# Chunked attention feeding an ELU network: the later tiles' attention as 64x64x64 products in four quarters of the array

## The chip, the cores and the metric

The kernel runs on one core of one Trainium2 chip. What is compared is the device time of one execution in microseconds (us), as the median of several. Beside it stands one execution that the hardware profiler took: when each engine worked, and what released it when it waited. TensorE (PE in the profile) multiplies matrices out of SBUF into the banks of PSUM; PEld is its weight load. VectorE (DVE), ScalarE (ACT) and GpSimd (POOL) do the elementwise work, and SyncE (SP) issues the DMAs.

## The reference

Attention runs inside chunks of 64 tokens: eight batches, eight heads, 576 tokens, head size 64. Its result, 4608 tokens by 512, goes through a two-layer network with an ELU between.

```python
q_c, k_c, v_c = [t.reshape(B, H, 9, 64, 64) for t in (q, k, v)]
scores = (1 / 8) * q_c @ k_c.transpose(0, 1, 2, 4, 3)
scores = scores - max(scores, axis=-1)
attn = exp(scores)
attn = attn / (sum(attn, axis=-1) + 1e-9)
x = (attn @ v_c) laid out as 4608 tokens x 512
h = x @ w_in                                   # 512 x 2048
g = where(h > 0, h, exp(min(h, 0)) - 1)
out = g @ w_out                                # 2048 x 512
```

## The kernel before

**Tiles and blocks.** A tile is 128 tokens, two chunks of 64. There are 36 tiles in nine blocks of four. The attention of the first four tiles runs at the start, that of the next four during block 0 (`early_tile`); both turn q, k and the attention weights with TensorE. The 28 others are the *later tiles* (`later_tile`): their q and k arrive by DMA in an order in which VectorE's 32x32 transposes turn them, and no TensorE transpose is needed. The attention of a tile is prepared one to two tiles ahead of the block that uses it.

**The network.** In blocks 0 to 2 (`hidden`, `elu`, `project`) each product is three products of float32r parts (high by high, high by low, low by high), all recorded at the helper's line L406. From block 3 on (`Pair`) two columns of `w_in` tiles are done at once by seven products instead of eight (`p1` to `p7`), whose operands were written to `a_dram` and are loaded again for every pair. Its parts are written as `o<-wo_hi,wi_hi` (second layer) and `h<-...` (first layer) in the profile.

**A later tile, step by step.** `attention_tile` is a generator; each `yield` ends a step, and the strings `LATER` and `PAIRS` say where a step stands (`n` a step of the following tile, `a` a step of the present one). The steps are these.

- VectorE turns q into `qT` (L283) and k into `k_apart` (L286), the latter in two instructions of 64 partitions each: head 2h in the upper half of the rows, head 2h+1 in the lower half, in separate columns, and zeros elsewhere.
- *Scores* (L357): for each pair of heads and each chunk one product with 128 rows, 64 output partitions and 128 columns. The zeros of `k_apart` keep the two heads apart. Eight products for a tile.
- The maximum `mx` (L363) and the subtraction (L377) on VectorE, the exponential (L381) on ScalarE, the sum, its inverse and the scaling (L383 to L316) on VectorE.
- Eight DMAs (L328) within SBUF bring `ah` into `aq`, and two VectorE transposes of 64 partitions (L333) put it into `a_apart`, which is zero where the chunks would mix.
- *Products by v* (L341): for each head one product with 128 rows, 64 output partitions and 128 columns. Eight for a tile.
- ScalarE copies the result out of PSUM into `xf` (`keep_x`, L392).

Scores and products by v each take a bank of their own from the pool `ps_a` of two. In nearly every tile the scores of the next tile and the products by v of the present one follow each other on TensorE.

**What sets the order.** All four engines run in the order in which the program is written (`manual_schedule`); waits are semaphores that the framework adds.

Of the kernel before, what the change touches and what calls it, by code (L numbers as in the profile page):

```python
# [10 lines left out]
F32 = mybir.dt.float32  # L11
# [9 lines left out]
def kernel(  # L21
# [59 lines left out]
    a_apart = const.tile([P, H, P], F32, name="a_apart")  # L81
# [178 lines left out]

    def front_tensor(q_sb, k_sb, kbd, at, psum):
# [16 lines left out]
        yield qT  # L278

    def front_vector(qk, kbd, at):  # L280
        yield
        qT = at.tile([P, NK, P], F32, name="qT")
        nc.vector.transpose(out=qT.rearrange("p h (t u) -> p h u t", u=4), in_=qk[:, 0])  # L283
        for j in range(2):
            js = slice(j * D, (j + 1) * D)
            nc.vector.transpose(  # L286
                out=kbd[js, :, j, :].rearrange("p h (t u) -> p h u t", u=4), in_=qk[js, 1]
            )
        yield qT
# [23 lines left out]
    def back_vector(a, z, v_sb, at, psum):  # L313

        ah = wst.tile([P, 2, H, Q], F32, name="y")
        nc.vector.tensor_tensor(  # L316
            out=ah.rearrange("p e h k -> p h e k"),
            in0=a.rearrange("p h (e k) -> p h e k", e=2),
            in1=z.rearrange("p h (e k) -> p h e k", e=1).broadcast_to([P, H, 2, Q]),
            op=ALU.mult,  # L320
        )
        yield
        aq = wst.tile([P, 2, H, Q], F32, name="y")
        for c in range(2):
            for e in range(2):
                for u in range(2):
                    p0, n0 = c * C + e * Q, c * C + u * Q
                    nc.sync.dma_start(out=aq[p0:p0 + Q, u], in_=ah[n0:n0 + Q, e])  # L328
        yield

        for c in range(2):
            cs = slice(c * C, (c + 1) * C)
            nc.vector.transpose(  # L333
                out=a_apart[cs, :, cs].rearrange("p h (u t) -> p h u t", u=2),
                in_=aq[cs].rearrange("p u h k -> p h u k"),
            )
        yield
        x_ps = psum([P, NK, P])
        for h in range(H):
            hp, j = divmod(h, 2)  # L340
            nc.tensor.matmul(  # L341
                x_ps[j * D:(j + 1) * D, hp, :], lhsT=v_sb[:, h, :], rhs=a_apart[:, h, :],
                start=True, stop=True,
            )
        return x_ps

    def attention_tile(tt: int, front, back, v_sb, kbd, at, psum, put, by_head: bool = False):
# [38 lines left out]
        x_ps = yield from back(a, z, v_sb, at, psum)  # L386
        yield
        put((slice(None), slice(None), slice(tt * P, (tt + 1) * P)), x_ps)
        yield
# [338 lines left out]
    with (  # L728
# [17 lines left out]
        for tt in range(NTT):  # L746
            psum = psum_of(ps_start)
            front = front_tensor(loaded[f"q{tt}"], loaded[f"k{tt}"], kbds[tt], start, psum)
            tiles.append(attention_tile(
                tt, front, back_tensor, loaded[f"v{tt}"], kbds[tt], start, psum, split_x  # L750
            ))
# [9 lines left out]
    ps_a = ctx.enter_context(tc.tile_pool(name="ps_a", bufs=2, space=bass.MemoryType.PSUM))  # L761
# [3 lines left out]
    psum = psum_of(ps_a)  # L765
# [19 lines left out]
    upcoming, second_products = None, []  # L785
# [6 lines left out]
    def early_tile(n: int):  # L792
# [4 lines left out]
        return attention_tile(  # L797
            n % NTT, front, back_tensor, load_v(n0, io), k_apart, at, psum, keep_x, by_head=True
# [11 lines left out]
    def later_tile(n: int, qk, v_sb):  # L810
        front = front_vector(qk, k_apart, at)
        return attention_tile(n % NTT, front, back_vector, v_sb, k_apart, at, psum, keep_x)
# [162 lines left out]
```

## Time and profile before

| | us |
|---|---|
| median of 3 runs | 890.68 (890.2 to 891.88) |
| the profiled execution | 890.75 |
| its span, first to last instruction | 889.0 |
| mean granted TensorE clock | 0.998 |
| VectorE busy | 554.5 |
| ScalarE busy | 486.2 |
| 28 transposes of q (L283) | 30.9 |
| 56 half transposes of k (L286) | 61.3 |
| 56 half transposes of the weights (L333) | 39.3 |

The first three rows differ by what lies around the span: 890.75 less 889.0 is 1.75 us before the first and behind the last instruction. A row of the profile gives an instruction's engine, its line, what it writes and reads, its shape, how often, and how long. A TensorE shape such as `128*64 128x128` means 128 rows of the array, 64 output columns of it, and a result of 128 columns. One product of float32 operands is issued as two matmul instructions (and two weight loads): 28 later tiles with eight products by v are 448 instructions at L341. The recorded length of a matmul is longer than its share of the array, since matmuls overlap; what counts is the distance between starts.

### The profile page before, as it was taken

The page shows a single profiled execution, that of the slowest core. Times are in us where ns is not written, and L with a number is a line of the kernel's source. Part 1 is how long each engine was busy: PE and PEld are TensorE (multiplying, and loading weights), DVE is VectorE, ACT ScalarE, POOL GpSimd, SP SyncE. Part 2 cuts the span into 40 slices and gives each one's busy share as a digit, 9 for nine tenths or more (in the row PEclk, how much of TensorE's full clock was granted, in tenths as well). Part 3 has the DMA queues.
Part 4 walks back from the last instruction along what each step waited for, and adds up shares of the span by engine and source line. Part 5 has one row for each costly group of instructions (what it writes and reads, how often), then busy time and mean ns, then how long its engine had stood idle before and what let it go on. Part 6 is the DMA issues. An engine that isn't in the chain of part 4 may idle for free.

```text
span 889.0 us, 15432 instructions
## 1 busy us (share of the span) xinstructions
PE 869.5 (98%) x5726; PEld 750.1 (84%) x5726; DVE 554.5 (62%) x859; ACT 486.2 (55%) x931; POOL 232.1 (26%) x196
## 2 busy tenths in 40 slices
PE   7899999999999999999999999999999999999997
PEld 6678887888888878888888888888888888888996
DVE  5899878567756586557655675567556755543222
ACT  5899984444544346455644564456444654465443
POOL 2000005114223023223422351226222622253221
PEclk9999999999999999999999999999999999999999
DMA  8775552545466758777689769876868688467521
GB/s 203 203 259 178 183 133 92 169 140 177 129 201 218 216 169 263 238 236 228 203 259 295 238 190 270 255 212 196 282 204 258 198 272 254 153 209 234 166 83 49
DMA packets 156700, 180.35 MB, mean 203 GB/s; under 512 B 67024, under 2 KB 123344, under 8 KB 156624
## 3 DMA queue, kind: packets, MB, share of 16 engines
q1 hardware_dynamic: 156624, 179.36, 65.9%
q8 instruction: 45, 0.74, 0.3%
q14 instruction: 31, 0.25, 0.1%
HBM read 147.85 MB, written 24.12 MB: 193 GB/s over the span
## 4 chain that ended last, share of the span: by engine, by line
PE 84%; DVE 5%; DMA 3%; SPq 2%; issue 2%; ACT 2%; POOL 1%; DVEq 0%; POOLq 0%; ACTq 0%
PE o L406 39%; PE h L406 37%; PE ps_a L357 3%; PE ps_a L341 3%; DMA st<-in_moe_w_out_dram 2%; DVE t L577 2%; SPq L230 1%; SPq L219 1%; POOL wi_lo L628 1%; POOL wi_lo L572 1%; DVE k_apart L286 1%; DVE e L620 0%; SPq L119 0%; DVE a L377 0%; DVE e L426 0%
## 5 line engine op out<-in xcount | busy, mean ns | idle before, releaser
L628 POOL TENSOR_TENSOR wi_lo<-e,wi_hi 128x512 fp32r<-128x512 f32 x94 | 123.2, 1311 | 336.8 <-ACT wi_hi L625 336.8
L406 PE MATMUL h<-xhi,wi_hi 128*128 128x256 f32 (+1 forms) x704 | 189.4, 315 | 1.4 <-DVE e L426 0.8
L613 DVE TENSOR_TENSOR kept<-h,kept 128x256 f32<-128x256 f32 x144 | 60.9, 423 | 169.5 <-PE h L406 122.1
L608 ACT COPY kept<-h 128x256 f32<-128x256 f32 x192 | 70.2, 366 | 168.1 <-PE h L406 167.9
L406 PE MATMUL o<-wo_lo,wi_hi 128*128 128x512 f32 x384 | 152.4, 397 | 0.0
L406 PE MATMUL o<-wo_hi,wi_hi 128*128 128x512 f32 x384 | 152.2, 396 | 0.0
L406 PE MATMUL o<-wo_hi,wi_lo 128*128 128x512 f32 x384 | 150.0, 390 | 1.0 <-POOL wi_lo L628 1.0
L406 PE MATMUL h<-xlo,wi_hi 128*128 128x256 f32 (+1 forms) x448 | 147.1, 328 | 0.0
L406 PEld LDWEIGHTS h<-xhi,wi_hi 128*128 128x128 f32 x704 | 123.6, 188 | 18.4 <-issue 4.3
L406 PE MATMUL h<-xhi,wi_lo 128*128 128x256 f32 (+1 forms) x448 | 131.4, 330 | 0.2 <-DVE wi_lo L160 0.2
L620 DVE SCALAR_TENSOR_TENSOR e<-e,kept 128x512 f32<-128x512 f32 x96 | 70.7, 736 | 38.7 <-ACT e L618 36.4
L406 PEld LDWEIGHTS h<-xlo,wi_hi 128*128 128x128 f32 x448 | 84.3, 188 | 12.0 <-DVE xlo L399 0.2
L406 PEld LDWEIGHTS h<-xhi,wi_lo 128*128 128x128 f32 x448 | 79.8, 188 | 11.9 <-issue 1.0
L406 PEld LDWEIGHTS h<-wi_lo,wi_hi 128*128 128x128 f32 x576 | 81.5, 189 | 9.5 <-ACT kept L608 1.0
L406 PEld LDWEIGHTS o<-wo_hi,wi_lo 128*128 128x128 f32 x384 | 72.3, 188 | 18.7 <-POOL wi_lo L628 2.7
L617 ACT ACTIVATE e<-kept 128x512 f32<-128x512 f32 x96 | 60.6, 632 | 48.7 <-DVE kept L613 41.8
L406 PE MATMUL h<-wi_lo,wi_hi 128*128 128x256 f32 x576 | 84.6, 282 | 0.3 <-ACT kept L608 0.3
L481 POOL TENSOR_TENSOR kept<-wi_hi,wi_lo 128x512 f32<-128x512 f32 x16 | 20.3, 1293 | 221.7 <-DVE qT L283 136.7
L406 PE MATMUL o<-wo_hi,ghi 128*128 128x512 f32 x192 | 76.4, 398 | 0.0
L406 PEld LDWEIGHTS o<-wo_lo,wi_hi 128*128 128x128 f32 x384 | 73.5, 191 | 2.3
L406 PE MATMUL o<-wo_hi,glo 128*128 128x512 f32 x192 | 75.0, 391 | 0.0
L406 PE MATMUL o<-wo_lo,ghi 128*128 128x512 f32 x192 | 74.9, 390 | 0.0
(90 smaller groups left out, 1444.8 us busy)
## 6 DMA issues: line engine op xcount, KB each, us to landing
wi_hi<-a_dram SPq DMA_DIRECT2D x128, 448.0 KB, 5.5
wi_lo<-a_dram SPq DMA_DIRECT2D x64, 448.0 KB, 5.7
kept<-in_q_dram SPq DMA_DIRECT2D x100, 128.0 KB, 7.0
kept<-in_k_dram SPq DMA_DIRECT2D x100, 128.0 KB, 5.2
st<-in_moe_w_in_dram SPq DMA_DIRECT2D x16, 512.0 KB, 4.2
st<-in_moe_w_out_dram SPq DMA_DIRECT2D x16, 512.0 KB, 4.9
a_dram<-kept SPq DMA_DIRECT2D x16, 512.0 KB, 4.1
y<-y SPq DMA_DIRECT2D x224, 32.0 KB, 1.9
```

The source lines that it names most:

```text
L219: nc.sync.dma_start(out=dst[p0:p0 + n], in_=src[b, :, s0:s0 + n, :].rearrange("h s d -> s h d"))
L230: nc.sync.dma_start(out=v_sb[j * C:(j + 1) * C, :, c, :], in_=v[b, j::2, ss, :].rearrange("h s d -> s h d"),)
L341: nc.tensor.matmul(x_ps[j * D:(j + 1) * D, hp, :], lhsT=v_sb[:, h, :], rhs=a_apart[:, h, :], start=True, stop=True,)
L357: nc.tensor.matmul(s_ps[cs, 2 * hp:2 * hp + 2, :], lhsT=qT[:, hp, cs], rhs=kbd[:, hp, :, cs], start=True, stop=True,)
L406: nc.tensor.matmul(ps, lhsT=a, rhs=b, start=start, stop=stop, skip_group_check=onto)
L481: nc.gpsimd.tensor_tensor(out=out, in0=a, in1=b, op=op)
L577: nc.vector.tensor_tensor(out=to, in0=a, in1=b, op=ALU.subtract)
L608: nc.scalar.copy(out=out, in_=self.x)
L613: nc.vector.tensor_tensor(out=out, in0=self.y, in1=self.kept[kept], op=ALU.add)
L617: nc.scalar.activation(out=e, in_=c, func=AF.Relu, scale=-1.0)
L620: nc.vector.scalar_tensor_tensor(out=e, in0=e, scalar=-1.0, in1=c, op0=ALU.add, op1=ALU.max)
L628: engine.tensor_tensor(out=glo, in0=e, in1=ghi.bitcast(F32), op=ALU.subtract)
```

## The change

The later tiles get a generator of their own, `later_attention`; the early ones keep theirs under the name `early_attention`, with the same instructions.

- k is turned by one transpose of 128 partitions into a dense `kT` (in the memory of `k_apart`), without zeros.
- The scores are sixteen products of 64 rows, 64 output partitions and 64 columns. They go round the four quarters of the array: (row half, output half) = (0,0), (1,1), (0,1), (1,0).
- The attention weights are turned by one transpose of 128 partitions into `turned`. `a_apart` and its memset go.
- The products by v are sixteen products of the same size over the same quarters.
- `ps_a` is one tile of two banks. A product whose rows are the upper half of the array writes the first bank, the others the second. The scores take columns 0 to 255 of both banks, the products by v columns 256 to 511. `banks[0]` is the tile last taken, so a tile's products by v stand in the banks that the next tile's scores took just ahead of them.
- Heads are kept in the order even, odd within `a` and `turned`, and the copy to `xf` reads from the two banks (128x2x4x64 in place of 128x4x128).

```diff
-    a_apart = const.tile([P, H, P], F32, name="a_apart")
+    turned = const.tile([P, H, C], F32, name="turned")
...
-    def front_vector(qk, kbd, at):
...
-    def back_vector(a, z, v_sb, at, psum):
...
+    def later_attention(tt: int, qk, v_sb):
+        halves = [slice(i * C, (i + 1) * C) for i in range(2)]
+        quarters = [(0, 0), (1, 1), (0, 1), (1, 0)]
+        yield
+        qT = at.tile([P, NK, P], F32, name="qT")
+        kT = k_apart.rearrange("p h j t -> p (h j) t")[:, :NK, :]
+        for i, to in enumerate((qT, kT)):
+            nc.vector.transpose(out=to.rearrange("p h (t u) -> p h u t", u=4), in_=qk[:, i])
+        yield
+        banks[:] = [ps_a.tile([P, 2, DM], F32, name="ps_a")]
+        scores = banks[0][:, :, :NK * C].rearrange("p j (h t) -> p j h t", h=NK)
+        for hp in range(NK):
+            for j, c in quarters:
+                nc.tensor.matmul(
+                    scores[halves[c], j, hp, :], lhsT=qT[halves[j], hp, halves[c]],
+                    rhs=kT[halves[j], hp, halves[c]], start=True, stop=True,
+                )
+        yield
+        mx = sm.tile([P, 2, NK, 1], F32, name="mx")
+        nc.vector.tensor_reduce(out=mx, in_=scores, axis=AX.X, op=ALU.max)
+        a = at.tile([P, H, C], F32, name="a")
+        nc.vector.tensor_tensor(
+            out=a.rearrange("p (j h) t -> p j h t", j=2), in0=scores,
+            in1=mx.broadcast_to([P, 2, NK, C]), op=ALU.subtract,
+        )
+        yield
...
+        nc.vector.transpose(
+            out=turned.rearrange("p h (u t) -> p h u t", u=2), in_=aq.rearrange("p u h k -> p h u k")
+        )
+        yield
+        x_ps = banks[0][:, :, NK * C:].rearrange("p c (h t) -> p c h t", h=NK)
+        for hp in range(NK):
+            for c, j in quarters:
+                nc.tensor.matmul(
+                    x_ps[halves[j], c, hp, :], lhsT=v_sb[halves[c], 2 * hp + j, :],
+                    rhs=turned[halves[c], j * NK + hp, :], start=True, stop=True,
+                )
+        yield
+        nc.scalar.copy(
+            out=xf[:, :, tt * P:(tt + 1) * P].rearrange("p h (c t) -> p c h t", c=2), in_=x_ps
+        )
+        yield
...
+        if blk == 1:
+            early.close()
+            ps_a = ctx.enter_context(
+                tc.tile_pool(name="ps_a", bufs=1, space=bass.MemoryType.PSUM))
```

TensorE in the middle of block 3, before: the last second-layer products of one pair, scores of the next tile, products by v of the present one, and the first product of the next pair.

```order
L406 MATMUL o_3211<-wo_hi,wi_hi 128x512
L406 MATMUL o_3211<-wo_lo,wi_hi 128x512
L406 MATMUL o_3211<-wo_hi,wi_lo 128x512
L357 MATMUL ps_a<-k_apart,qT 64x128 x8
L341 MATMUL ps_a<-a_apart,v_sb 64x128 x8
L406 MATMUL h<-xhi,wi_hi 128x256
L406 MATMUL h<-xlo,wi_hi 128x256
```

The same place after the change (line numbers have moved; L432 is the helper that was L406).

```order
L432 MATMUL o_3325<-wo_hi,wi_hi 128x512
L432 MATMUL o_3325<-wo_lo,wi_hi 128x512
L432 MATMUL o_3325<-wo_hi,wi_lo 128x512
L365 MATMUL ps_a<-k_apart,qT 64x64 x16
L407 MATMUL ps_a<-turned,v_sb 64x64 x16
L432 MATMUL h<-xhi,wi_hi 128x256
L432 MATMUL h<-xlo,wi_hi 128x256
```

The steps stand where they stood; each has sixteen products of half the columns and half the rows in place of eight.

VectorE at the end of block 2, before, with what each instruction waits for (`PE`, `Activation`, `DMAHW` are the semaphores of TensorE, ScalarE and the DMA queues): the transposes of one tile's weights, four differences of x (L577), the transposes of q and k of the next tile, one ELU step, and the maximum of the next tile's scores.

```order
L333 STREAM_TRANSPOSE a_apart<-y 64x8x64 [waits DMAHW2_49,DMAHW7_49,DMAHW1_49,DMAHW0_49]
L333 STREAM_TRANSPOSE a_apart<-y 64x8x64 [waits DMAHW5_49,DMAHW6_49,DMAHW4_49,DMAHW3_49]
L577 TENSOR_TENSOR t<-xf 128x2x128
L577 TENSOR_TENSOR t<-xf,t 128x2x128 [waits DVE_49] x2
L577 TENSOR_TENSOR t<-xf 128x2x128
L283 STREAM_TRANSPOSE qT<-kept 128x4x4x32
L286 STREAM_TRANSPOSE k_apart<-kept 64x4x4x32 x2
L426 SCALAR_TENSOR_TENSOR e<-e,h 128x512 [waits Activation_49]
L363 TENSOR_REDUCE mx<-ps_a 128x8 [waits PE_49]
```

The same place after the change.

```order
L400 STREAM_TRANSPOSE turned<-y 128x512 [waits DMAHW4_49,DMAHW5_49,DMAHW3_49,DMAHW6_49,DMAHW2_49,DMAHW7_49,DMAHW1_49,DMAHW0_49]
L603 TENSOR_TENSOR t<-xf 128x2x128
L603 TENSOR_TENSOR t<-xf,t 128x2x128 [waits DVE_49] x2
L603 TENSOR_TENSOR t<-xf 128x2x128
L359 STREAM_TRANSPOSE qT<-kept 128x4x4x32
L359 STREAM_TRANSPOSE k_apart<-kept 128x4x4x32
L452 SCALAR_TENSOR_TENSOR e<-e,h 128x512 [waits Activation_49]
L371 TENSOR_REDUCE mx<-ps_a 128x8 [waits Activation_49]
```

Two transposes fewer stand ahead of the scores, the transpose of the weights waits for all eight DMAs at once, and the maximum waits for ScalarE (its copy of the products by v out of the same banks) in place of TensorE.

More of the change, by code (lines that the diff above doesn't have):

```diff
@@ L278, in front_tensor @@
         yield qT
-    def front_vector(qk, kbd, at):
[L281 to L289, printed above, removed]
     def back_tensor(a, z, v_sb, at, psum):
@@ L311, in back_tensor, with early_attention @@
         return x_ps
-    def back_vector(a, z, v_sb, at, psum):
[L315 to L347, printed above, removed]
+    def early_attention(tt: int, front, v_sb, kbd, at, psum, put, by_head: bool = False):
         next(front)
@@ L385, in attention_tile @@
         nc.vector.reciprocal(z, z)
-        x_ps = yield from back(a, z, v_sb, at, psum)
+        x_ps = yield from back_tensor(a, z, v_sb, at, psum)
         yield
         put((slice(None), slice(None), slice(tt * P, (tt + 1) * P)), x_ps)
+        yield
[25 more added lines that the diff above has]
+        yield
+        nc.scalar.activation(out=a, in_=a, func=AF.Exp, scale=SCALE)
+        yield
+        z = sm.tile([P, H, 1], F32, name="z")
+        nc.vector.tensor_reduce(out=z, in_=a, axis=AX.X, op=ALU.add)
+        nc.vector.tensor_scalar_add(z, z, 1e-9)
+        nc.vector.reciprocal(z, z)
+        ah = wst.tile([P, 2, H, Q], F32, name="y")
+        nc.vector.tensor_tensor(
+            out=ah.rearrange("p e h k -> p h e k"),
+            in0=a.rearrange("p h (e k) -> p h e k", e=2),
+            in1=z.rearrange("p h (e k) -> p h e k", e=1).broadcast_to([P, H, 2, Q]),
+            op=ALU.mult,
+        )
+        yield
+        aq = wst.tile([P, 2, H, Q], F32, name="y")
+        for c in range(2):
+            for e in range(2):
+                for u in range(2):
+                    p0, n0 = c * C + e * Q, c * C + u * Q
+                    nc.sync.dma_start(out=aq[p0:p0 + Q, u], in_=ah[n0:n0 + Q, e])
+        yield
+        nc.vector.transpose(
+            out=turned.rearrange("p h (u t) -> p h u t", u=2), in_=aq.rearrange("p u h k -> p h u k")
+        )
+        yield
+        x_ps = banks[0][:, :, NK * C:].rearrange("p c (h t) -> p c h t", h=NK)
[5 more added lines that the diff above has]
+                )
+        yield
+        nc.scalar.copy(
+            out=xf[:, :, tt * P:(tt + 1) * P].rearrange("p h (c t) -> p c h t", c=2), in_=x_ps
+        )
@@ L760 @@
     ps_o = ctx.enter_context(tc.tile_pool(name="ps_o", bufs=1, space=bass.MemoryType.PSUM))
[L761 to L765 removed]
+    early = ctx.enter_context(ExitStack())
+    ps_early = early.enter_context(
+        tc.tile_pool(name="ps_early", bufs=2, space=bass.MemoryType.PSUM))
+    psum = psum_of(ps_early)
     pending, acts = [], {}
```

14 lines of the change are left out of this document (6 added, 8 removed).

## The prediction

> **What bounds the kernel now.** I read first the page's busy shares, the granted clock and the chain that ended last.
>
> ```profile
> PE 869.5 (98%) x5726; PEld 750.1 (84%) x5726; DVE 554.5 (62%) x859; ACT 486.2 (55%) x931; POOL 232.1 (26%) x196
> PEclk9999999999999999999999999999999999999999
> PE 84%; DVE 5%; DMA 3%; SPq 2%; issue 2%; ACT 2%; POOL 1%; DVEq 0%; POOLq 0%; ACTq 0%
> ```
>
> TensorE is busy 98% of the span at full clock, and the chain runs through it for 84%. Whatever shortens the queue of TensorE shortens the kernel, unless the next instruction then waits. What its groups waited for, over the whole span, is little:
>
> ```profile
> L406 PE MATMUL h<-xhi,wi_hi 128*128 128x256 f32 x512 | 113.3, 284 | 1.3 <-DVE e L426 0.8 <-DVE kept L613 0.6
> L406 PE MATMUL o<-wo_hi,wi_lo 128*128 128x512 f32 x384 | 150.0, 390 | 1.0 <-POOL wi_lo L628 1.0
> L357 PE MATMUL ps_a<-k_apart,qT 128*64 128x128 f32 x512 | 35.0, 279 | 1.8 <-DVE k_apart L286 1.4 <-issue 0.4
> L341 PE MATMUL ps_a<-a_apart,v_sb 128*64 128x128 f32 x448 | 29.3, 273 | 0.5 <-POOL kept L481 0.5
> ```
>
> So the question is what the two attention steps of the 28 later tiles take of TensorE's queue now, and what they will take. The timeline of TensorE in block 3 shows one pair of steps with their neighbours; the columns are start, length from the first start to the last end, and the number of instructions.
>
> ```profile
> 407.71 0.40 PE L406 MATMUL o<-wo_lo,wi_hi 128*128 128x512 f32 x1
> 407.95 0.39 PE L406 MATMUL o<-wo_hi,wi_lo 128*128 128x512 f32 x1
> 408.27 1.09 PE L357 MATMUL ps_a<-k_apart,qT 128*64 128x128 f32 x16
> 409.19 1.04 PE L341 MATMUL ps_a<-a_apart,v_sb 128*64 128x128 f32 x16
> 410.17 0.38 PE L406 MATMUL h<-xhi,wi_lo 128*128 128x256 f32 x1
> 410.39 0.28 PE L406 MATMUL h<-xlo,wi_lo 128*128 128x256 f32 x1
> ```
>
> From the end of the last `o` product to the usual pace of the `h` products this is about 2.1 us in every tile.
>
> **The change: the size of a step.** What a quarter's product costs is shown by the early tiles, whose products by v (L307) are already 64x64x64, though in two quarters only, the two on the diagonal. The source view gives the lengths of single instructions (least, median, most), and the timeline one such step.
>
> ```profile
> L341 PE MATMUL ps_a<-a_apart,v_sb x448: 272/273/324, 153.6 to 782.7; 128*64 128x128 f32 x150
> L307 PE MATMUL ps_a<-qT,v_sb x256: 217/218/363, 18.2 to 131.2; 64*64 64x64 f32 x128
> 104.29 0.39 PE L406 MATMUL h<-xhi,wi_lo 128*128 128x512 f32 x1
> 104.61 1.15 PE L307 MATMUL ps_a<-qT,v_sb 64*64 64x64 f32 x32
> 105.69 0.50 PE L406 MATMUL o<-wo_hi,ghi 128*128 128x512 f32 x1
> ```
>
> *Now.* Sixteen instructions in 1.04 us; less the last one's 0.273 that is 0.767 us for the starts. They start two at a time, in the two output halves, so there are seven distances of 0.767 / 7 = 0.1096 us, and a step is worth 8 x 0.1096 = 0.877 us. The scores' row is 0.05 longer because it comes behind another shape.
>
> *Two quarters.* Of L307's 1.15 us I take the same 0.05 and the last one's 0.218 away: 0.882 us, fifteen distances of 0.0588 us, two matmuls in each. That the two are from different quarters and run at once is seen where data came late:
>
> ```profile
> 23.32 0.30 PE L307 MATMUL ps_a<-qT,v_sb 64*64 64x64 f32 x2 [1.75 <-DMA v_sb<-in_v_dram]
> 23.65 0.27 PE L307 MATMUL ps_a<-qT,v_sb 64*64 64x64 f32 x2
> 130.31 0.27 PE L307 MATMUL ps_a<-qT,v_sb 64*64 64x64 f32 x1
> ```
>
> At 23.32 a single product had its data. Its two instructions follow each other: 0.30 us is longer than one (0.218). At 23.65 two more products were free, and two matmuls fit in 0.27 us, which is the length of one alone at the head of a step (130.31): they started within some 0.01 us of each other. They are the first halves of two products, and the second of these stands in the program behind the first one's second half. So TensorE goes past an instruction whose quarter is taken and starts another quarter's.
>
> *Four quarters.* The changed step has 16 products, 32 instructions. If all four quarters run at once, they stand in 8 groups of four, each as long as a quarter needs for one instruction, 0.0588 us: 0.470 us. This saves 0.877 - 0.470 = 0.407 us a step; with 28 tiles of two steps, 56 x 0.407 = **22.8 us**. No row shows four at once, so I bound the group: it is no shorter than 0.0588, the time of one quarter by itself, and no longer than 0.1176, when two quarters wait for the other two; then a step takes 16 x 0.0588 = 0.941 us and costs 0.064 us more than now. I take the lower end: the row at 23.65 shows the lookahead, and the halves differ in nothing that the two rows together do not show at work, output halves over the same rows (L341) and different rows with different outputs (L307).
>
> The change of shape around the steps costs the same. From the last wide product to the first small one are 0.32 us in both rows (407.95 to 408.27, 104.29 to 104.61). On the way out 409.19 + 0.877 = 410.07 is 0.10 us short of 410.17, and 104.61 + 0.05 + 16 x 0.0588 = 105.60 is 0.09 short of 105.69.
>
> **Two tiles are different.** At the end of block 2 TensorE waits for the transposes of k:
>
> ```profile
> 319.58 0.39 PE L406 MATMUL o<-wo_hi,glo 128*128 128x512 f32 x1
> 321.38 1.09 PE L357 MATMUL ps_a<-k_apart,qT 128*64 128x128 f32 x16 [1.41 <-DVE k_apart L286]
> 315.13 1.42 DVE L333 STREAM_TRANSPOSE a_apart<-y 64x512 f32<-64x512 f32 x2
> 318.16 1.09 DVE L283 STREAM_TRANSPOSE qT<-kept 128x512 f32<-128x512 f32 x1
> 319.10 2.14 DVE L286 STREAM_TRANSPOSE k_apart<-kept 64x512 f32<-64x512 f32 x2
> ```
>
> VectorE works without a gap from 315.13 to here. One of two k transposes goes; the other now has 128 partitions, which costs nothing, as q's takes 1.09 with 128 and k's half 1.07 with 64. By the same reason one of two weight transposes goes, 0.71. So `kT` is there 1.78 us earlier, before TensorE can start at 319.58 + 0.32 = 319.90. The step begins 321.38 - 319.90 = **1.5 us** earlier.
>
> The second later tile loses:
>
> ```profile
> 152.01 1.09 PE L357 MATMUL ps_a<-k_apart,qT 128*64 128x128 f32 x16
> 153.59 1.09 PE L341 MATMUL ps_a<-a_apart,v_sb 128*64 128x128 f32 x16 [0.49 <-POOL kept L481]
> 152.63 0.71 DVE L333 STREAM_TRANSPOSE a_apart<-y 64x512 f32<-64x512 f32 x1 [0.67 <-DMA y<-y]
> ```
>
> Its products by v wait for the transpose that ended at 153.34, which waited for a DMA until 152.63 (GpSimd, named by the row, is not what they read). `turned` waits for all eight DMAs, so it also starts at 152.63 and ends at the same time; the scores' 0.4 us saved here become a longer wait: **+0.4 us**.
>
> **The rest lies beside TensorE.** VectorE loses 1.09 + 0.71 us in each tile, 50 us in all; it is busy 62%, so this pays only where TensorE waits for it, as above. If the transposes cost more for their strides, the bound is the 1.78 us that they now take together. The memset of `a_apart` leaves an idle GpSimd. The copy to `xf` moves the same 128x512 elements.
>
> The new wait stands on VectorE: `mx` follows ScalarE's copy, with the subtraction and ELU steps queued behind. Block 2 has the nearest rows:
>
> ```profile
> 250.06 0.68 DVE L363 TENSOR_REDUCE mx<-ps_a 128x8 f32<-128x512 f32 x1
> 250.28 0.58 ACT L392 COPY xf<-ps_a 128x512 f32<-128x512 f32 x1 [0.86 <-PE ps_a L341]
> 322.52 0.69 DVE L363 TENSOR_REDUCE mx<-ps_a 128x8 f32<-128x512 f32 x1 [0.56 <-PE ps_a L357]
> 323.39 0.59 ACT L392 COPY xf<-ps_a 128x512 f32<-128x512 f32 x1 [0.78 <-PE ps_a L341]
> ```
>
> Today the copy ends 0.80 us behind the start of `mx` in the first place and 1.46 in the second. It will come 0.81 us earlier (two steps of 0.407), which covers the first; in the second 0.65 us of waiting stays, in a tile that begins 1.5 us earlier. I cost it at nothing; without that cover it is 0.65 us on VectorE, once.
>
> **Sum**, against the profiled execution of 890.75 us (its span is 889.0; it lies within 0.1 us of the median, 890.68): 890.75 - 22.8 - 1.5 + 0.4 = **866.9 us**.
>
> **The rivals.**
>
> *Two at a time.* TensorE keeps only two quarters in flight, by lookahead or by the paths of the rows that two quarters share. Then 56 x 0.064 = +3.6 us, less the 1.5 us at block 2 (the +0.4 goes): 892.9 us, slower. It decides as soon as a group of four takes longer than 0.877 / 8 = 0.1096 us. For it: no row shows three matmuls at once. Against it: the rows at 23.32 and 23.65.
>
> *A least distance of starts, whatever the quarter.* The densest row, L307, has 32 instructions in 0.941 us, 0.0294 each. If that were a floor, the step is the same 0.941 us and the time 892.9 us too; below 0.877 / 32 = 0.0274 it gains, and at 0.0147 it no longer binds. Against it: the two that start within some 0.01 us of each other at 23.65.
>
> The Trainium skill has a rule of this kind that speaks against the change: "TensorEngine Tiling (Array Packing)", section Performance Considerations, gives each matmul an overhead of about 60 cycles and warns against taking a tiling factor from a dimension that is already small; "TensorE: Matmul & The Clock Gate", section Back-to-back issue gap, puts the floor up to 64 columns at about 25 ns. If it held over all quarters, 32 of them would make an estimated 0.80 us a step, and the time about 885 us. The trace agrees within a quarter (0.0588 us is above it) and not between two (0.01 at 23.65); no run here shows four.
>
> *Given back in part.* Groups of four between 0.06 and 0.10 us, or waits that the faster TensorE meets. The tightest is the second layer's wait for GpSimd's `wi_lo` (1.0 us in all, in the rows above). At 0.08 a step takes 0.64, and 56 x 0.237 = 13.3 us are saved: 890.75 - 13.3 - 1.5 + 0.3 = 876.3 us. Against it: VectorE, which stands ahead of these waits, gets 50 us less to do, and ScalarE and GpSimd are busy 55% and 26%.
>
> **How the numbers follow.** Four at once 0.72: 866.9 us, with a range of its own from 864.0 (the three small waits of the first rows, 0.8 + 0.6 + 1.0 = 2.4 us, go too, and half a microsecond of reading) to 871. Given back in part 0.14: 871 to 885. A floor of starts 0.05. Two at a time 0.09. The range 864.0 to 883.0 leaves out the last two and the tail of the third, some 0.18. What a measurement tells from no change here is about 0.2%, 1.8 us. Faster: 0.72 + 0.14 and a part of the floor's, 0.87; the same 0.04, from pairs that cost as little as the 1.5 us gained; slower 0.09.
>
> **What would show it.** The rows of the new steps: 32 instructions in about 0.47 + 0.16 us (0.05 more in the scores), 0.47 us from the scores' first start to the products' (0.52 with the shape change), and the next `h` product 1.2 us behind the scores' start where it is now 1.9. A row of 1.15 us as L307's now means two at a time. The wait of 1.41 us for `k_apart` is gone, the one ahead of the second tile's products is longer. I am wrong if the steps shrink and the span does not: then a wait for POOL, ACT or DMA stands behind them that is not in the rows above.

## The result, and the profile after

| | before | after |
|---|---|---|
| median, us | 890.92 (890.2 to 891.88, 4 runs) | 870.57 (869.68 to 870.96, 4 runs) |
| the profiled execution, us | 890.75 | 869.68 |
| its span, us | 889.0 | 867.9 |

The ratio is 0.977, with a 95% interval of 0.975 to 0.979: faster by 20.4 us. The prediction said 866.9 us, in a range of 864.0 to 883.0.

From the page of the changed kernel, the busy times:

```profile
PE 848.3 (98%) x6622; PEld 731.1 (84%) x6622; DVE 504.5 (58%) x803; ACT 484.4 (56%) x931; POOL 235.6 (27%) x195
```

TensorE's busy time fell by 21.2 us and the span by 21.1. VectorE's fell by 50.0. The groups of lines on TensorE, each shape by itself, with the idle time ahead of them in the last columns:

```profile
L432 PE MATMUL h<-xhi,wi_hi 128*128 128x256 f32 x512 | 113.6, 284 | 2.8 <-DVE e L452 2.3 <-DVE kept L639 0.4
L365 PE MATMUL ps_a<-k_apart,qT 64*64 64x64 f32 x896 | 19.5, 224 | 0.0
L407 PE MATMUL ps_a<-turned,v_sb 64*64 64x64 f32 x896 | 18.2, 219 | 0.7 <-DVE turned L400 0.7
```

The waits of the scores (1.8 us before) are gone; there are 2.3 us for VectorE's `e` now, all of it in one wait, and 0.7 for `turned`. One pair of steps in block 3, on TensorE's timeline:

```profile
399.49 0.39 PE L432 MATMUL o<-wo_hi,wi_lo 128*128 128x512 f32 x1
399.81 0.69 PE L365 MATMUL ps_a<-k_apart,qT 64*64 64x64 f32 x32
400.33 0.65 PE L407 MATMUL ps_a<-turned,v_sb 64*64 64x64 f32 x32
400.90 0.39 PE L432 MATMUL h<-xhi,wi_lo 128*128 128x256 f32 x1
```

From the last `o` product to the next `h` product it is 1.41 us, where it was 2.22 (407.95 to 410.17). This is 0.81 less for the two steps, and it comes in 24 of the 29 places where these steps stand. In the other five the same stretch shrank by 0.40 us (the first and the last, with one step each), 1.13 (the second), 2.29 (where block 2 ends) and 0.02 (the step at 445 us). All 29 together make 23.57 us. The span fell by 21.10; the other 2.47 us were lost between the step where block 2 ends and the next one. From the second wide product behind the one to the last ahead of the other TensorE took 15.53 us before and takes 18.00 now. What else differs cancels to some 0.05 us: these steps begin 0.39 us earlier, which is ahead of anything that the change touches, and the stretch behind the last of them is 0.23 shorter; the stretch from 334 to 355 us is 0.49 longer, for a reason that is not shown, and small differences make 0.18.

So two places stay to be explained, and I call them **the border** (314 to 333 us, block 2 to block 3) and **the step at 445** (scores of the fifteenth later tile, products by v of the fourteenth; the expectations below call it the fifteenth tile's). TensorE at the border, and two cuts of the whole core there (the columns are each engine's busy us with its count, then the granted clock, the DMA share and GB/s):

```profile
320.36 0.39 PE L432 MATMUL o<-wo_hi,glo 128*128 128x512 f32 x1
323.07 0.36 PE L432 MATMUL h<-xhi,wi_hi 128*128 128x256 f32 x1 [2.33 <-DVE e L452]
...
326.24 0.63 PE L432 MATMUL o<-wo_hi,ghi 128*128 128x512 f32 x1
326.67 0.63 PE L432 MATMUL o<-wo_lo,ghi 128*128 128x512 f32 x1
```

```profile
320.00:324.00 4.00, 1.67 (x11) 1.23 (x10) 3.24 (x5) 1.66 (x4) 2.41 (x2) 1.00 0.15 41
324.00:328.00 4.00, 4.00 (x16) 3.19 (x15) 4.00 (x6) 2.33 (x6) 2.54 (x3) 0.58 0.10 27
```

The same wait before the change, on the same timeline:

```profile
330.54 0.36 PE L406 MATMUL h<-xhi,wi_hi 128*128 128x256 f32 x1 [0.75 <-DVE e L426]
```

It was 0.75 us and is 2.33. Behind the longer one the clock is granted at 0.58 for 4 us, and 512-column products start 0.43 us apart instead of 0.23. What TensorE waits for is the `e` at the end of this queue on VectorE:

```profile
312.46 0.67 DVE L452 SCALAR_TENSOR_TENSOR e<-e,h 128x512 f32<-128x512 f32 x1
315.04 0.69 DVE L371 TENSOR_REDUCE mx<-ps_a 128x8 f32<-128x512 f32 x1 [1.90 <-ACT xf L412]
...
319.91 1.51 DVE L603 TENSOR_TENSOR t<-xf 128x256 f32<-128x256 f32 x1
321.45 0.88 DVE L603 TENSOR_TENSOR t<-xf,t 128x256 f32<-128x256 f32 x2
322.25 0.68 DVE L452 SCALAR_TENSOR_TENSOR e<-e,h 128x512 f32<-128x512 f32 x1
```

From `mx` to this `e` VectorE takes 7.21 us, and it took 7.20 before (322.52 to 329.72). But `mx` starts 1.85 us behind the scores' first start, where it was 1.14, since it waits for ScalarE's copy. And TensorE comes to the place 0.80 us sooner, since its two steps are shorter. 0.71 + 0.80 is 1.51 of the 1.58 us by which the wait grew. The other 0.89 of the 2.47 us are what is left of the lower clock's cost behind the wait.

### The profile page after: what moved, and what is told of

Same layout as the page of the kernel before. It is cut to its first block, busy times and chain, and to the rows that moved or that the text cites. A ratio compares the mean times of both kernels' runs of the same rounds, so it can differ in the third digit from the quotient of the medians.

```text
span 867.9 us, 17156 instructions
## 1 busy us (share of the span) xinstructions
PE 848.3 (98%) x6622; PEld 731.1 (84%) x6622; DVE 504.5 (58%) x803; ACT 484.4 (56%) x931; POOL 235.6 (27%) x195
## 4 chain that ended last, share of the span: by engine, by line
PE 85%; DVE 4%; SPq 3%; DMA 3%; issue 2%; POOL 1%; ACT 1%; POOLq 0%; DVEq 0%
PE o L432 41%; PE h L432 39%; PE ps_a L365 2%; PE ps_a L407 2%; DVE t L603 1%; DMA wi_hi<-a_dram 1%; SPq L230 1%; DMA q_sb<-in_q_dram 1%; SPq L219 1%; POOL wi_lo L654 1%; POOL wi_lo L598 1%; DVE e L646 1%; PE ps_a L266 1%; PE ps_a L297 0%; DVE a L373 0%
## 5 line engine op out<-in xcount | busy, mean ns | idle before, releaser
L432 PE MATMUL h<-xhi,wi_hi 128*128 128x256 f32 (+1 forms) x704 | 189.7, 315 | 2.8 <-DVE e L452 2.3
L432 PE MATMUL o<-wo_lo,wi_hi 128*128 128x512 f32 x384 | 152.3, 397 | 0.0
L432 PE MATMUL o<-wo_hi,wi_hi 128*128 128x512 f32 x384 | 152.0, 396 | 0.0
L432 PE MATMUL o<-wo_hi,wi_lo 128*128 128x512 f32 x384 | 150.0, 391 | 1.0 <-POOL wi_lo L654 1.0
L432 PE MATMUL h<-xlo,wi_hi 128*128 128x256 f32 (+1 forms) x448 | 147.3, 329 | 0.1
L432 PEld LDWEIGHTS h<-xhi,wi_hi 128*128 128x128 f32 x704 | 124.0, 189 | 17.7 <-ACT wi_lo L597 2.7
L432 PE MATMUL h<-xhi,wi_lo 128*128 128x256 f32 (+1 forms) x448 | 131.4, 330 | 0.0
L432 PEld LDWEIGHTS h<-xlo,wi_hi 128*128 128x128 f32 x448 | 84.5, 189 | 12.5 <-DVE xlo L425 0.6
L432 PEld LDWEIGHTS h<-wi_lo,wi_hi 128*128 128x128 f32 x576 | 82.1, 190 | 9.0 <-POOL wi_lo L598 0.8
L432 PEld LDWEIGHTS h<-xhi,wi_lo 128*128 128x128 f32 x448 | 79.8, 188 | 10.7
L432 PEld LDWEIGHTS o<-wo_hi,wi_lo 128*128 128x128 f32 x384 | 72.2, 188 | 19.0 <-POOL wi_lo L654 3.1
L432 PE MATMUL h<-wi_lo,wi_hi 128*128 128x256 f32 x576 | 85.1, 283 | 0.0
L507 POOL TENSOR_TENSOR kept<-wi_hi,wi_lo 128x512 f32<-128x512 f32 x16 | 21.2, 1349 | 214.2 <-DVE qT L359 154.3
L432 PE MATMUL o<-wo_hi,ghi 128*128 128x512 f32 x192 | 76.6, 399 | 0.0
L651 ACT CAST wi_hi<-e 128x512 fp32r<-128x512 f32 x96 | 59.8, 623 | 29.6 <-DVE e L646 29.2
L432 PEld LDWEIGHTS o<-wo_lo,wi_hi 128*128 128x128 f32 x384 | 73.5, 191 | 2.3
L432 PE MATMUL o<-wo_hi,glo 128*128 128x512 f32 x192 | 75.4, 393 | 0.0
```

The costliest lines, as they stand in the source:

```text
L432: nc.tensor.matmul(ps, lhsT=a, rhs=b, start=start, stop=stop, skip_group_check=onto)
L507: nc.gpsimd.tensor_tensor(out=out, in0=a, in1=b, op=op)
L651: nc.scalar.copy(out=ghi, in_=e)
```

## The experiments

The theories: **A**, the maximum's wait for the copy is what costs the 2.47 us. **B**, the border is fixed by VectorE's and GpSimd's other work, and TensorE only arrives sooner. **C**, formed after the first runs: what is gained at the border is taken back at the step at 445, because the transfers there are issued late. Three more runs test how the four quarters come to run at once, and one whether VectorE's 50 us count.

### The maximum ahead of the copy

```diff
-        "n n H e e e P n a a n e n",
+        "n n H e e e P n a n e n a",
```

> One place is edited: where block 2 ends, VectorE's maximum and subtraction of the next tile stand ahead of ScalarE's copy of this tile's products, so the copy waits and not the maximum. Theory A (the maximum's wait of 1.90 us for the copy pushes VectorE's queue back until TensorE waits 2.33 us for it at 323 us, and the pause drops the clock to 0.58 for 4 us): the maximum starts about 313.9 instead of 315.04, TensorE's wait falls to about 1.2 us, the clock stays near 1.0 in the stretch after it, and the time falls by 1.1 + 1.7 = 2.8 us, to about 867.8; by 1.1 alone (869.5) if the shorter pause still costs the clock. Theory B (TensorE only arrives earlier at a border that VectorE's and GpSimd's other work fixes): the wait stays near 2.3 us and the time within 0.4 us of 870.6.

Measured: 870.51 us (868.86 to 871.4), ratio 0.978 (0.976 to 0.980): not to be told from the changed kernel. Three rows of its trace, VectorE's maximum, TensorE's wait, and the step at 445:

```profile
315.75 0.69 DVE L371 TENSOR_REDUCE mx<-ps_a 128x8 f32<-128x512 f32 x1 [1.28 <-PE ps_a L407]
```

```profile
323.84 0.36 PE L432 MATMUL h<-xhi,wi_hi 128*128 128x256 f32 x1 [1.76 <-DVE e L452]
...
445.01 0.69 PE L365 MATMUL ps_a<-k_apart,qT 64*64 64x64 f32 x32
447.55 0.69 PE L407 MATMUL ps_a<-turned,v_sb 64*64 64x64 f32 x32 [1.84 <-DVE turned L400]
```

```profile
324.00:328.00 4.00, 4.00 (x26) 3.36 (x26) 3.62 (x5) 2.32 (x6) 2.42 (x3) 1.00 0.13 37
```

A wait of 1.28 for the products by v stands in the place of 1.90 for their copy, so only half of what A asked for is gained. But the wait is down to 1.76 us, the clock stays at 1.00, and the border takes 16.38 us instead of 18.00: 1.62 us gained. Of these, 0.57 are the shorter wait; the rest goes with the clock, and that the shorter wait is what kept the clock up is not shown (the run with two heads in a row, below, kept it behind a wait of 2.30 us). Then the products at 445 start 2.54 us behind their scores, where it was 1.25: 1.29 us lost again. A has the place and a part of the cost; its sum does not come out.

### The elu earlier

```diff
-        "H xB11 n xt1b xt2b xt4b e xB21 n xT2 e e e R",
+        "H xB11 n e e xt1b xt2b xt4b xB21 n xT2 e e R",
```

> One place is edited: in the last step of block 2 the ScalarE and VectorE part of the elu that frees the h bank is issued ahead of three subtractions t<-xf on VectorE. By theory A and by theory B alike the bank is free by about 320.6 us, the 2.33 us wait is gone, the clock stays near 1.0 in the 4 us after it: 2.3 + 1.7 = 4.0 us less, about 866.6. If the subtractions, 0.65 us later each, are waited for in turn by TensorE, 0.7 to 2 us of it comes back (867.3 to 868.6); if the drop of the clock has another cause than the pause, it stays and the gain is 2.3 at most.

Measured: 870.06 us (868.98 to 872.33), ratio 0.978 (0.976 to 0.980). The wait of 2.33 us is gone, as expected, but two others came:

```profile
324.90 0.50 PE L432 MATMUL o<-wo_hi,ghi 128*128 128x512 f32 x1 [1.05 <-ACT ghi L457]
326.29 0.50 PE L432 MATMUL o<-wo_hi,glo 128*128 128x512 f32 x1 [0.66 <-DVE glo L460]
```

The later steps of the same elu now stood behind the subtractions and the casts that need them. The border takes 18.00 us as before the edit, and the clock drops here too. Neither A nor B foresaw this: at the border several chains end within a microsecond or two of each other.

### The four quarters: one quarter after the other

```diff
-        for hp in range(NK):
-            for j, c in quarters:
+        for j, c in quarters:
+            for hp in range(NK):
```

(and the same in the products by v.)

> Only the order of the 32 instructions of each step changes: the four heads of one quarter in a row, then the next quarter, where the changed kernel takes the four quarters in turn. If products start strictly in program order and one quarter holds one product at a time, a step lasts 32 x 0.0588 = 1.88 us instead of 0.47, and the time rises by 56 x 1.41 = 79 us to about 950. If TensorE lets a product pass one that waits for its quarter, and looks far enough ahead for it (eight instructions, those of one quarter), the step stays near 0.47 and the time near 870.6. A short look ahead (two to four instructions) gives something between, 890 to 930.

Measured: 911.47 us (910.95 to 911.79), ratio 1.024 (1.022 to 1.026). The order alone turns the gain into a loss of 20 us against the kernel before. TensorE's timeline at one pair of steps:

```profile
393.72 1.36 PE L365 MATMUL ps_a<-k_apart,qT 64*64 64x64 f32 x29
394.87 0.27 PE L407 MATMUL ps_a<-turned,v_sb 64*64 64x64 f32 x1
394.93 0.22 PE L365 MATMUL ps_a<-k_apart,qT 64*64 64x64 f32 x1
394.98 0.22 PE L407 MATMUL ps_a<-turned,v_sb 64*64 64x64 f32 x1
394.99 0.22 PE L365 MATMUL ps_a<-k_apart,qT 64*64 64x64 f32 x1
395.04 0.22 PE L407 MATMUL ps_a<-turned,v_sb 64*64 64x64 f32 x1
395.04 0.22 PE L365 MATMUL ps_a<-k_apart,qT 64*64 64x64 f32 x1
```

The first product by v, of another quarter, starts while three score instructions that stand ahead of it in the program have not started: these follow at 394.93, 394.99 and 395.04, 0.058 us apart. So instructions do pass each other, and it is three that can be passed. Within the step each quarter's first start lies 5 to 6 ns behind the fifth of the eight of the quarter before. A step takes 1.319 us from its first to its last start, between the two ends of the expectation, as a short look ahead should.

### The four quarters: two heads of a quarter in a row

```diff
+        for j, c, hp in [(j, c, hp) for two in ((0, 1), (2, 3)) for j, c in quarters for hp in two]:
```

> Order only: two heads of a quarter in a row, then the next quarter. In the run with four heads in a row each new quarter started 5 ns behind the fifth of the eight instructions of the quarter before it, so three were still waiting and the new one was the fourth. Theory: TensorE looks over four instructions that have not started, and a product is two instructions. Stepping through the order by that rule (58.5 ns between two starts in one quarter, 6.5 ns between any two, 49 ns more at the first of a quarter) gives 0.68 to 0.73 us from the first to the last start of a step, against 0.477 now: 56 x 0.20 to 0.25 = 11 to 14 us more, 882 to 885. A look over three gives 0.86 to 0.91 (892 to 895), over eight 0.54 (874). If what counted was the run of eight in one quarter and not the look ahead, no change (870.6).

Measured: 872.36 us (871.86 to 873.17), ratio 0.979 (0.978 to 0.980). A step takes 0.54 to 0.57 us, and four different quarters start within 40 ns, 13 ns apart, though four instructions of each stand in a row. My rule of four instructions over all quarters falls. A look over eight fits here (0.54), but stepped through for one quarter after the other it would have given 0.98 us and not 1.319. What comes near both runs is a place for three waiting instructions in each quarter, beside the one that runs; the first that finds no place holds back everything behind it. Stepped through with starts 58.4 ns apart in a quarter (107 at the first), this gives 0.477 us for the order of the change, 0.497 for this one and 1.314 for one quarter after the other; measured were 0.477, 0.54 to 0.57 and 1.319. The rule is made to fit after the runs, and for this order it gives 0.04 to 0.07 too little.

This run also parts the wait at the border from the clock. The same `e` is waited for as long as in the changed kernel, and the clock stays up:

```profile
323.98 0.35 PE L430 MATMUL h<-xhi,wi_hi 128*128 128x256 f32 x1 [2.30 <-DVE e L450]
```

```profile
324.00:328.00 4.00, 4.00 (x25) 3.39 (x26) 3.48 (x5) 2.32 (x6) 2.42 (x3) 1.00 0.16 43
```

The border takes 16.91 us here, 1.09 less than the 18.00 with the clock down. So the lower clock costs some 1.1 us at this border, and a wait of 2.3 us does not always bring it. The other three executions of this kernel have a mean clock of 0.996 to 0.997 where the profiled one has 1.000, so it differs between executions, too.

### The scores alone

```diff
+        x_ps = banks[0][:, :, NK * C:].rearrange("p b (h t) -> p b h t", h=2)
+        for h in range(H):
+            hp, j = divmod(h, 2)
+            nc.tensor.matmul(x_ps[halves[j], hp // 2, hp % 2, :], lhsT=v_sb[:, h, :],
+                             rhs=a_apart[:, j * NK + hp, :], start=True, stop=True)
```

> The scores are computed as in the changed kernel; the products by v again as eight 128x64x128 matmuls over the zero-padded weights, with the two half transposes for them. If the gain is per step and the same in both: 28 steps go back from 0.47 to 0.87 us, +11.3 us, about 882, and the gain where block 2 ends (the scores there wait for one transpose of k, not two) stays. If the gain there came from the products' part, 1.5 us more, about 883.5. If the four quarters only overlap across the two adjoining steps, much more is lost than half: over 886.

Measured: 885.53 us (883.23 to 885.8), ratio 0.994 (0.992 to 0.996). All three guesses missed it; the step shows by what:

```profile
407.29 0.69 PE L365 MATMUL ps_a<-k_apart,qT 64*64 64x64 f32 x32
407.92 1.09 PE L408 MATMUL ps_a<-a_apart,v_sb 128*64 128x128 f32 x16
408.94 0.39 PE L433 MATMUL h<-xhi,wi_lo 128*128 128x256 f32 x1
```

The products by v take 1.09 us again, 0.05 more than the 1.04 that they took behind scores of their own shape, and come 0.63 us behind the scores' start where two steps of the small shape lie 0.52 apart (0.11 more). The pair of steps is 0.25 us shorter than before, not 0.40: the one change of shape between them takes 0.15 us, and 28 x 0.15 = 4.2 us is what the first guess lacked. The step where block 2 ends keeps its gain of the k transposes, and the border behind it takes 17.99 us, as in the changed kernel, with the same wait (2.32 us). So a gain at that step is lost in the border without the new products by v, too.

### VectorE's transposes in halves

```diff
-        for i, to in enumerate((qT, kT)):
-            nc.vector.transpose(out=to.rearrange("p h (t u) -> p h u t", u=4), in_=qk[:, i])
+        nc.vector.transpose(out=qT.rearrange("p h (t u) -> p h u t", u=4), in_=qk[:, 0])
+        for js in halves:
+            nc.vector.transpose(out=kT[js].rearrange("p h (t u) -> p h u t", u=4), in_=qk[js, 1])
```

(and `turned` likewise.)

> The matmuls stay as in the changed kernel; VectorE turns k and the weights in two halves of 64 partitions again, as before: 28 x (1.07 + 0.7) = 50 us more work on VectorE. If that work lies beside TensorE, as the prediction says: the scores where block 2 ends wait 0.5 us for the second half of k, the products of the second and of the fifteenth tile wait 0.7 us longer for theirs, nothing else: 1.2 to 1.9 us more, 871.8 to 872.5. If VectorE's shorter queue is part of what each step gained (TensorE's waits for VectorE in the pairs), 0.1 us or more per tile on top: over 874.5. Back at 890 if the gain was VectorE's altogether.

Measured: 873.4 us (872.5 to 875.71), ratio 0.980 (0.979 to 0.982). VectorE is busy 553.7 us again. The scores where block 2 ends wait twice for k:

```profile
314.27 0.30 PE L367 MATMUL ps_a<-k_apart,qT 64*64 64x64 f32 x2 [0.32 <-DVE k_apart L360]
315.29 0.63 PE L367 MATMUL ps_a<-k_apart,qT 64*64 64x64 f32 x27 [0.72 <-DVE k_apart L360]
```

This step becomes 1.39 us longer; the second tile's 0.35 and the step at 445 0.22. All the others are the same to 0.002 us, so the 50 us of VectorE lie beside TensorE, as predicted. The steps make 1.96 us of the 2.8 that it is slower; the time lies above the 872.5 that the first case allowed and under the 874.5 of the second, and where the other 0.8 come from is open.

### The border's work in another order

```diff
-        "n n H e e e P n a a n e n",
-        "H xB11 n xt1b xt2b xt4b e xB21 n xT2 e e e R",
+        "n n H e e e P n a n e n a",
+        "H xB11 e xt1b xt2b e xT2 e e n xt4b xB21 n R",
```

> Where block 2 ends: the maximum ahead of the copy, and in the last step the elu that frees the h bank and the subtractions that TensorE's next products need go ahead of the next tile's sums and weights on VectorE. Theory C (the border costs 2.33 us of waiting and 1.7 us of halved clock, but what is gained there is given back where the fifteenth tile's weights are turned, because they wait for eight transfers that SP issues only by about 444 us behind sixteen loads of tokens): the wait at 323 us is under 0.5 us, the clock stays at 1.0, TensorE is 3.5 to 4.5 us ahead at 440 us, and 3 to 3.5 us of this are lost before the products at 446 us, whose gap grows from 0.78 to about 4 us: about 869.5 in all. Theory A without C: the gain stays, 866 to 867.

Measured: 870.58 us (869.67 to 871.33), ratio 0.977 (0.976 to 0.978). The clock stays at 1.00, and the wait at 323 is replaced by two others:

```profile
323.40 0.39 PE L432 MATMUL h<-xlo,wi_hi 128*128 128x256 f32 x1 [1.28 <-POOL xlo L598]
...
333.94 0.69 PE L407 MATMUL ps_a<-turned,v_sb 64*64 64x64 f32 x32 [1.36 <-DVE turned L400]
```

The tile's sums and weights, put behind, came too late for its own products by v one step on. C's number for the step at 445 was wrong as well: its gap stayed at 0.69 us. Here the border's gain does not get that far.

### The transfers of the weights ahead of the tokens

What C says is read from SP's queue ahead of the step at 445 in the changed kernel (start, length of the run of issues, count):

```profile
424.00 4.90 SPq L247 DMA_DIRECT2D kept<-in_q_dram  x8
428.94 4.62 SPq L247 DMA_DIRECT2D kept<-in_k_dram  x8
433.67 1.36 SPq L219 DMA_DIRECT2D v_sb<-in_v_dram  x2
435.12 0.57 SPq L481 DMA_DIRECT2D out_dram<-k_sb  x1
435.74 1.46 SPq L566 DMA_DIRECT2D wi_hi<-a_dram  x3
437.29 7.14 SPq L398 DMA_DIRECT2D y<-y  x8
```

The weights `y` were ready on VectorE at 431.4 us. Their transfers wait till 437.29, behind q and k of a tile whose two chunks lie in different batches, which takes sixteen loads; other tiles take eight. The tile period is 22.4 us (23.2 before the change), and in this one SP issues for 20 of them. Two rows of the same queue in the run with the maximum first:

```profile
423.74 6.27 SPq L247 DMA_DIRECT2D kept<-in_q_dram  x8
...
437.51 7.94 SPq L398 DMA_DIRECT2D y<-y  x8
```

They contradict the first half of C. TensorE's step ahead of these loads begins at 422.58 us in the changed kernel and at 422.31 with the maximum first, and SP's first load follows 1.43 us behind it in both. So SP's queue moves with TensorE, and a gain at the border brings the loads forward as well. What made the 1.29 us is that from the first load to the last transfer of the weights SP took 21.70 us in that execution and 20.42 in the changed kernel's; why it took longer is not shown. The second half of C stands: at this tile SP's run of issues is too long for the shorter period.

```diff
-        "n a a L p1 c1 ... c4 A w Q p3 d3 "
+        "n a a p1 c1 ... d2 A w n L Q Q p4 c4 A w Q p3 d3 "
```

> Only the place of the token loads in SP's order changes, in the pairs from block 3 on: behind the eight transfers of the weights and no longer ahead of them. By theory C the gap ahead of the products at 446 us falls from 0.776 to 0.038 us, nothing else moves: 0.74 us less, about 869.8. If the loads of the wide operands that then come behind the tokens are waited for, it is slower, by the 5 us that they are later per tile less their slack.

Measured: 920.87 us (919.96 to 921.17), ratio 1.033 (1.032 to 1.035). The gap at this step did fall to 0.044 us. But the tokens came too late, as a row of VectorE's timeline shows, and one of TensorE's:

```profile
427.03 1.09 DVE L359 STREAM_TRANSPOSE qT<-kept 128x512 f32<-128x512 f32 x1 [5.76 <-DMA kept<-in_q_dram]
```

```profile
430.51 0.58 PE L432 MATMUL h<-xhi,wi_hi 128*128 128x256 f32 x1 [3.98 <-DVE kept L639]
```

VectorE runs in order: its transpose waits for q, and the sum of partial products behind it, for which TensorE waits, waits too. Together with the border's other order:

> Both edits. By theory C they add up to more than the parts: the border's 3.5 to 4.5 us and the 0.74 us at the fifteenth tile stay gained, 865.3 to 866.3. If the fifteenth tile is late for another reason than SP's order (the transfers themselves), about 869 to 870, as with the border alone.

Measured: 925.88 us (923.74 to 928.05), ratio 1.039 (1.037 to 1.041), 5.0 us slower still than with the tokens late alone. Why is not shown; with the tokens late, the run tells nothing of C.

### The transfers on two queues

```diff
-                    nc.sync.dma_start(out=aq[p0:p0 + Q, u], in_=ah[n0:n0 + Q, e])
+                    queue = nc.scalar if c else nc.sync
+                    queue.dma_start(out=aq[p0:p0 + Q, u], in_=ah[n0:n0 + Q, e])
```

> Four of the eight transfers that turn the weights of a tile are issued by ScalarE's queue, four still by SP's. Theory C (the fifteenth tile waits since SP issues the eight one after the other, 0.6 us each, behind sixteen loads): the last of them is issued about 2.2 us earlier, the gap ahead of the products at 446 us falls from 0.776 to 0.038 us and that ahead of the second tile's from 0.378 to about 0.04: 1.1 us less, 869.5. If issuing them costs ScalarE its place (it waits in order for VectorE's y, or takes 0.5 us for each), TensorE waits for what ScalarE does next: 28 x 0.3 to 2 us more, 879 or over. If the transfers themselves and not their issue are late: no change.

Measured: 916.72 us (913.63 to 919.94), ratio 1.029 (1.026 to 1.031). The second tile's gap fell to 0.038 us, but the one at 446, for which the edit was made, grew to 5.05. ScalarE lost its place, the second case of the expectation. Of the view of its waits (us in total, times, longest):

```profile
ACT e L450 <- DMA y<-y: 44.6, 8, 7.2
ACT kept L635 <- DMA y<-y: 31.9, 15, 2.5
```

With the maximum ahead of the copy as well:

> The two queues, and VectorE's maximum ahead of ScalarE's copy where block 2 ends. In the run with the maximum first alone, TensorE was 2.0 us ahead behind the border and lost 1.3 us of it before the fifteenth tile's products. By theory C that loss goes away here: the time is that of the two queues alone less 2.0 us, 867.5 if that is 869.5. If the border's gain is lost elsewhere, the same as the two queues alone.

Measured: 915.59 us (913.31 to 918.7), ratio 1.028 (1.025 to 1.030), the same; it tells nothing of C.

### The maximum first, and v behind the weights

```diff
-        "n a a L p1 c1 ... d2 A w n Q Q p4 c4 A w Q p3 d3 "
+        "n a a L p1 c1 ... d2 A w n V Q Q p4 c4 A w Q p3 d3 "
...
+                    elif item == "V":
+                        if n + 1 < NB * NTT:
+                            next_v["v"] = load_heads(v, "v_sb", (n + 1) * P, io)
```

> VectorE's maximum ahead of ScalarE's copy where block 2 ends, and in the pairs the load of v (needed 30 us later) behind the eight transfers of the weights in SP's order, so that these are issued 1.4 us earlier in the fifteenth tile; the loads of tokens stay where they are, and no engine's own order changes. By theory C the gap ahead of the products at 446 us is 0.7 us at most (2.05 us with the maximum first alone), and the time is 0.7 to 2.0 us under the changed kernel's: 868.6 to 869.9. If that tile is late by the transfers and not by their issue, the gap stays near 2 us and the time at 870.5.

Measured: 867.75 us (866.91 to 868.84, 5 runs), ratio **0.974** (0.973 to 0.975). This is 2.8 us under the changed kernel by the medians, and under the 868.6 that was expected at best; the two intervals touch (0.9754 and 0.9753). SP's queue and TensorE at the step at 445:

```profile
433.00 1.36 SPq L567 DMA_DIRECT2D wi_hi<-a_dram  x3
434.45 6.99 SPq L398 DMA_DIRECT2D y<-y  x8
441.54 1.35 SPq L219 DMA_DIRECT2D v_sb<-in_v_dram  x2
```

```profile
443.27 0.69 PE L365 MATMUL ps_a<-k_apart,qT 64*64 64x64 f32 x32
443.79 0.65 PE L408 MATMUL ps_a<-turned,v_sb 64*64 64x64 f32 x32
```

The transfers go out ahead of v, and the products follow their scores after 0.52 us, as in any tile. SP's first load again comes 1.42 us behind TensorE's step ahead of it (420.58 and 422.00), and from there to the last transfer of the weights SP now takes 19.44 us: 1.36 of the difference to the run with the maximum first are the two loads of v, the rest is the other loads and transfers, whose length differs from execution to execution. The border takes 16.37 us, as with the maximum first alone. So the two gains add up: the border's, and the end of the wait behind SP. The span is 865.1 us, 2.8 less than the changed kernel's, which is 1.63 at the border, 0.79 at this step, and 0.4 ahead of them, where runs of one kernel differ too.

Not tried: one bank for both row halves in place of two. Two products of different rows that write the same outputs would then write the same bank at once, in no set order. The Trainium skill says that different row tiles cannot use the same PSUM bank at the same time ("TensorEngine Tiling (Array Packing)", Gotcha 1: PSUM Pressure). No run here shows it.

## Why the prediction was right, and where not

*Four at once, 22.8 us: right.* A step is 0.477 us from first to last start, 0.403 less than before by the difference of the pairs of steps (0.805 to 0.806 in block 3, where 0.814 was predicted). The rivals *two at a time* and *a least distance of starts* fall with the 0.477: four quarters start within 20 ns. The estimate of 0.80 us a step, by the rule of the Trainium skill that the prediction weighed, falls with them. The reason given, that TensorE passes an instruction whose quarter is taken, is right too, but it is less than the prediction made of it: by the rule that comes nearest to the runs only three instructions of a quarter can wait, and the order of the quarters decides between 870 and 911 us. The prediction took the order for granted.

*The change of shape around the steps, at no cost: right.* The next `h` product comes 0.148 us behind the last start, and came 0.203 behind before; nothing more was lost. The sign of 1.2 us from the scores' start to this product was a slip of adding: its own terms give 0.52 + 0.47 + 0.10 = 1.09, and 1.09 was measured (399.81 to 400.90).

*The end of block 2, 1.5 us: right at its place, and lost behind it.* The step became 2.29 us shorter, 1.5 beyond its two steps' saving, and with k in halves it is 1.39 longer again. The step of the prediction that failed is the next one.

*`mx` behind the copy, costed at nothing: wrong.* The prediction put the cost at 0.65 us on VectorE, once, if the cover fails, and found the place; it measured 0.71. It did not follow VectorE's queue on to the `e` for which TensorE already waited 0.75 us. There the 0.71 and the 0.80 of the shorter steps became waiting, and behind the wait of 2.33 us the clock was down. The prediction counted from the profiled execution, and that one came to 869.68, 2.78 us over 866.9: 2.47 at this border, 0.79 at the step at 445, 0.24 because the other steps were shortened a little less than the 0.407 each, less 0.72 at the second later tile. That the 0.72 covers most of the 0.79 is luck. That `mx` is the cause at the border is shown in part: with the maximum first the wait is 0.57 us shorter and the border 1.62, of which the clock is about 1.1. The clock's part is not `mx`'s for certain, since with two heads in a row it stayed up behind a wait of 2.30 us. With the maximum first the border still takes 0.85 us more than before, about the 0.80 by which TensorE's shorter steps bring it there sooner; this much agrees with B. Two other orders moved the wait to other instructions.

*The second later tile, +0.4 us: wrong in sign.* The stretch became 1.13 us shorter, not 0.41: the landing of the transfers was held fixed at 152.63 us, but VectorE's `y` and with it the transfers also came earlier, and `turned` started at 151.31. The first transfer was issued at 144.65 us where it was 146.23: 0.39 of these 1.58 us are the earlier start of the steps, and ahead of `y` VectorE has one half transpose of k less to do (1.07).

*A wait that was not in the rows: the step at 445, +0.79 us.* The "given back in part" rival had the kind of it, but looked for it at GpSimd. It was SP's queue, which the prediction didn't read; the last experiment shows it: with v out of the way the wait is gone.

*VectorE's 50 us beside TensorE: right.* With the halves back 26 of the steps are the same to 0.002 us.

## What to carry to other kernels

Small products in quarters of the array pay only if few of one quarter stand in a row in the program: one at a time gave 870.6 us here, two 872.4, four 911.5. Where a change shortens the busiest engine, look for the places at which it already waits, and follow the waiting engine's queue up to there: at such a place the gain becomes waiting, and a longer wait can cost the clock as well. Read SP's queue like an engine's; where it issues for 20 of 22 us, a transfer that nobody needs soon belongs behind one that is waited for.

## What the runs showed of the hardware

- Instructions pass each other (products by v at 394.87 us ahead of scores at 394.93 to 395.04). The three orders come near a rule of three waiting instructions for each quarter beside the running one (1.314 us stepped through and 1.319 measured for one quarter after the other, 0.497 and 0.54 to 0.57 for two heads in a row). The Trainium skill has matmuls start and end strictly in program order, "TensorE: Matmul & The Clock Gate", section The mechanism; this trace differs in the starts, for float32 products of different quarters.
- A change between the 64-row and the 128-row shape inside a pair of steps cost 0.15 us.
- At the border a wait of TensorE of 2.33 us was followed by a clock of 0.58 over 4 us (it fell likewise with waits of 2.31 to 2.33 us there in five other runs), and one of 2.30 us was not (two heads in a row, 1.00 over the same 4 us). One of 1.76 us was not, in three runs; two of 1.05 and 0.66 us within 2.5 us were. So the length of one wait does not decide it. The Trainium skill warns of gaps over about 3 us ("TensorE: Matmul & The Clock Gate", section Why this matters for your kernels); here less was enough, in most of the runs and not in all.
